# Holding attention visits back while both chains of a product pair are open

## The chip, the cores and the metric

The kernel runs on one core of one Trainium2 chip. The metric is the device time of one execution in microseconds (us); lower is better. A core has five engines that run their own instruction streams side by side: TensorE (PE, the matrix products; its weight loads are listed apart as PEld), VectorE (DVE), ScalarE (ACT), GpSimd (POOL) and SyncE (SP, here a queue of transfers). They wait for each other through semaphores. What stands first in an engine's stream is run first: an instruction that waits holds up everything behind it on its engine.

## The reference

Squared-ReLU attention over 8 batches of 12 heads, 448 rows of 64, then a Fourier mixing with a residual, a normalization, and a feed-forward block (FFN) with a residual:

```python
scores = scale * np.matmul(q, k.transpose(0, 1, 3, 2))
attn = np.maximum(scores, 0.0) ** 2 / S
x = np.matmul(attn, v)                 # then heads side by side: 448 x 768 for each batch
mixed = np.real(np.fft.fft(np.fft.fft(x, axis=1), axis=2))
u = x + mixed
un = (u - mean) / np.sqrt(var + 1e-06)
out = u + np.maximum(un @ w_ch1, 0.0) @ w_ch2      # 768 -> 3072 -> 768
```

## The kernel before

Nothing in this kernel is written in its final order. Each stage is a Python generator that asks a planner (`Streams.run`, L102) for a piece of work: an engine, a duration, what it depends on, which buffers it takes and, if it likes, a condition `ok`. The planner keeps its own clock for each engine and always emits the request that can start first. A request whose condition does not hold sorts behind all that are free to go. It is still emitted when nothing else can be, and, once the FFN is two batches in (`sch.fill`, L2183), also where the best TensorE request would otherwise start over 0.5 planned us later than it. So a condition moves work; it is no wait on the chip. The result is a fixed order of instructions on each engine, with semaphores for the true dependencies alone.

The stages that matter here:

- **Attention** (`attention`, L834) comes as visits to TensorE. A full visit makes one head pair's value product from squared scores (seven matmuls, L822 and L827) and three blocks of new scores (six matmuls, L954). Each score block lies in one of three two-bank PSUM tiles (`BS`, psS), is read by ScalarE (L967, ReLU) and then squared by VectorE (L984) or ScalarE (L981). The values leave PSUM through VectorE or ScalarE into xT (L689, L686).
- **Mixing** of a finished batch: the channel transform (L1432), the row transform (L1240), and behind them sums, statistics and normalization on VectorE, ScalarE and POOL (L1275, L1284, L1303 on ScalarE or L1300 on POOL), stores, and transposed loads of the normalized rows (unT, L1380) on the SP queue.
- **FFN**, by groups of 256 rows from the fourth group on. The first product (L1930) runs as twelve blocks of twelve matmuls; each block fills one of the two remaining PSUM banks (`BF`, psF), which comes free when ScalarE (L1917) or VectorE (L1915) has applied the ReLU. The second product of a row pair saves one product in eight by sums and differences (`Pair`, L2031) and runs as **two chains**, `chain_a` (L2098) and `chain_b` (L2124), each a row of products of twelve matmuls (L2071) into one psF bank. Between two products of a chain, VectorE adds the bank to an output tile (L1623), and the next product of that chain waits for this addition. With both chains open, one runs its product while the other's addition is under way. Both psF banks are then held, so a visit's value product takes a psS tile, and the visit is cut to two score blocks. `chains[0]` counts the open chains: up by one in `first` (L2075) when a chain has its bank, down by one when it is through.
- The last four groups of 256 rows run as two joint stages (`joint`, L1733, products L1762), after the last attention visit; they have their own chains.

What sets the place of a visit is `gate` (L861). `progress[0]` is the FFN's position in batches, and `lead` the position that it must have reached before this visit: that of the visit less 2.9 batches, with a slope (L859, L860). From batch 2 on there must also be 1.3 us of planned FFN work between two visits with scores (`APART`).

Of the kernel before, what the change touches and what calls it, by code (L numbers as in the profile page):

```python
# [149 lines left out]
def need(eng, dur, deps=(), bufs=(), ok=None):  # L150
    return eng, dur, list(deps), list(bufs), ok


def mm(n):
    return n / 2400 + (0.002 if STAGE[0] else 0.006)
# [22 lines left out]
def kernel(  # L178
# [384 lines left out]
    progress, worked, visited = [0.0], [0.0], [-9.0]  # L563
    APART = 1.3
# [79 lines left out]
    tail = [0]  # L644
# [156 lines left out]
    chains, last_values = [0], Cell()  # L801

    def items(m):

        at = m // 2 * 7
        return [at, at + 1, at + 2, at + 3] if m % 2 == 0 else [at + 3, at + 4, at + 5, at + 6]

    def past(sets):

        return sets // 2 * 7 + sets % 2 * 3  # L810

    def turned_for(b, i):

        g, r = divmod(i, 7)
        return turned_at[b][g] if r == 3 else [turned_at[b][g][r > 3]]

    def value(av, i, m, sqs, start, stop, e):

        r = i % 7
        sq, _, home = sqs[i]  # L820
        if r == 3:
            nc.tensor.matmul(av[:, 0:S], lhsT=vn_home[:, (3 * H + 2 * m) * Dh:(3 * H + 2 * m + 2) * Dh], rhs=sq[:, m % 2, :], start=start, stop=stop,  # L822
                             skip_group_check=True)
        else:
            for h in range(2):
                at = (3 * (2 * m + h) + r % 4) * Dh
                nc.tensor.matmul(av[h * Dh:(h + 1) * Dh, 0:S], lhsT=vn_home[:, at:at + Dh], rhs=sq[:, h, :],  # L827
                                 start=start, stop=stop, skip_group_check=True)
        if r != 3 or m % 2:
            sqs.pop(i)  # L830
            sq_ids.append((e, home))
            BSQ.free.append(e)

    def attention(b, left=None):  # L834

        F, sqs, fresh = [], {}, []
        if b == ONE:
            yield need("ACT", 0.0, [], [BSQ] * 3)
            sq_left.t = max(t for t, i in sq_ids if i >= NSQ - 3)
            sq_ids[:] = [(t, i) for t, i in sq_ids if i < NSQ - 3]  # L840
        room = NSQ if b < ONE else NSQ - 3
        p = pa = pv = 0
        while pv < MC:
            if p == NB and pv == MC - 1 and 2 <= b < B - 1 and turned_at[b + 1][0][0].t is not None:
                return F, sqs
            few = b == 0 or progress[0] == 0.0
            n = min(1 if few else 3, NB - p)
            ma = pv

            lag = 3 if few else 1  # L850
            old = fresh[-lag] if len(fresh) >= lag else 0
            values = items(pv)[-1] < old if n else True
            n = max(0, min(n, room - (p - past(pv + values))))
            values = values or not n
            bv, mv, Fv, sv = b, ma, F, sqs
            if left is not None:
                values, bv, mv, (Fv, sv) = True, b - 1, MC - 1, left
            deps, bufs, dur, homes = [], [], 0.0, BF
            lead = b + ((p if n else pa) - (0 if left is None else 4)) / NB  # L859
            lead -= LEAD - SLOPE * (B - lead)  # L860
            gate = lambda: progress[0] >= lead and (b < 2 or worked[0] >= visited[0] + APART) and (b != 1 or tail[0] == 2 or tail[0] == 0 and p < 0)  # L861
            if values:
                deps += [sv[i][1] for i in items(mv)]
                if b > 1:
                    yield need("PE", 0.0, deps, [], gate)
                    if chains[0] == 2:
                        homes, n = BS, min(n, 2)
                bufs.append(homes)
                if b == 1:
                    deps.append(first_mixed)  # L870
                deps.append(ready[bv * NG + mv // 2][2])
                dur += 4 * mm(S) + SWITCH
            fresh.append(p + n)
            if n:
                now = sorted(range(p, p + n), key=lambda i: i % 7 == 3)
                deps += [c for i in now for c in turned_for(b, i)]
                bufs += [BS] * n
                last = [sum(1 + (j % 7 == 3) for j in now[x + 1:]) * mm(S) for x in range(n)]
                dur += (n + (now[-1] % 7 == 3)) * mm(S) + SWITCH
            e = yield need("PE", dur + SWITCH, deps, bufs, gate)  # L880
            av_end, scs = None, []
            if n:
                visited[0] = worked[0]

            for part in ("scores", "values") if few else ("values", "scores"):
                if part == "values" and values:
                    held = homes.take()
                    av = held[:, 0] if homes is BS else held
                    give = lambda when, homes=homes, held=held: homes.give(held, when)
                    order = sorted(items(mv), key=lambda i: i % 7 != 3)  # L890
                    for i in order:
                        value(av, i, mv, sv, i == order[0], i == order[-1], e)
                    av_end = e - (last[0] + mm(S) + SWITCH if n and not few else 0.0) + LATENCY["PE"]
                    if mv % 2 == 1:
                        BQ[2].free.append(e)
                    if bv == B - 1 and mv == MC - 1:
                        last_values.t = e + LATENCY["PE"]
                    if left is None:
                        pv += 1
                        pa = past(pv)  # L900
                if part == "values":
                    continue
                for x, i in enumerate(now if n else []):
                    sc = score(b, i)
                    scs.append((i, sc, e - SWITCH - (4 * mm(S) + SWITCH if values and few else 0.0) - last[x]))
                    if i % 7 == 6:
                        BQT.free.append(e)
            p += n
            for i, _, _ in scs:
                sqs[i] = [None, Cell(), None]  # L910
            if scs:
                sch.add(squares(b, scs, sqs), (0.2, 0.2))
            if av_end is not None:
                left = None
                yield from fold(bv, mv, Fv, av, give, av_end)
# [29 lines left out]
    def score(b, i):  # L945

        g, r = divmod(i, 7)
        qT, flat, (step, apart) = turned[b][g]
        sc = BS.take()
        for h in range(2):  # L950
            ps = slice(0, 128) if r == 3 else slice(h * Dh, (h + 1) * Dh)
            pair = h if r == 3 else r // 4
            k0 = r % 4 * step + pair * apart
            nc.tensor.matmul(sc[:, h, 0:S].rearrange("k (c q) -> k c q", c=4), lhsT=flat[ps, k0:k0 + KB],  # L954
                             rhs=qT[ps, pair], start=True, stop=True)
        return sc
# [519 lines left out]
    def mixes():  # L1476
        for b in range(B):
            yield from mix(b)
# [128 lines left out]
    def ffns():  # L1607
        for b in range(JOINTS[0]):
            yield need("SP", 0.0, [group_ready[b]])
            yield from ffn(b)  # L1610
        for n in range(len(JOINTS)):
            yield from joint(n)
# [544 lines left out]

    LEAD, MIXED, SPARE, ELASTIC = 2.9, 1, 0.5, (1, 99)
    SLOPE = 0.127
    with tc.manual_schedule():  # L2160
        small_constants()
        sch.engine.update(POOL=0.5, DVE=2.6)

        sch.add(loading(), (0, 4))
        sch.add(build_dft(), (0, 0.5))
        sch.add(turning((0,)), (0.05, 0.15))
        sch.add(ffns(), (4, 0))
        sch.add(mixes(), (1, 1))
        sch.add(first_attention(), (0, 0))
        for i in range(2):  # L2170
            sch.add(first_channels(i, range(MC - 1)), (5, 5))
        sch.add(attentions(), (3, 3))
        sch.add(warming(), (9, 9))
        sch.add(weight_sums(), (6, 6))
        sch.add(quarter_sums(), (6, 6))
        sch.add(halve(), (3, 3))
        sch.add(turns(), (1, 1))
        sch.add(turn_rest(), (2, 2))
        sch.add(root_table(), (0, 0.4))
        sch.add(negative(), (0, 0.35))  # L2180
        for slot in range(6):
            sch.add(outputs(slot), (4, 0))
        sch.fill = lambda: progress[0] > 2.0  # L2183
        sch.run()
# [30 lines left out]
```

## Time and profile before

| | |
|---|---|
| median of three runs | 569.09 us |
| the three runs | 569.48, 569.09, 566.94 us |
| profiled execution, first to last instruction | 566.4 us |
| TensorE busy | 556.5 us (98%), 4171 matmuls |
| VectorE busy | 436.2 us (77%) |
| ScalarE busy | 318.2 us (56%) |
| POOL busy | 195.9 us (35%) |

The profiled execution is one execution; its own length is known as the span alone, which leaves out what lies before its first and after its last instruction. Matmuls are pipelined, so that the listed durations of neighbours overlap: the time that one costs is read from the starts of neighbours. For example, a block of twelve matmuls of 384 columns takes 1.95 us from its start to the start of what follows, though each matmul is listed with 326 ns.

In the rows of the views, `L2071 PE MATMUL psF<-w,hT ... x12` stands for twelve matmuls of line 2071 that write psF and read w and hT; a bracket at the end of a row tells how long the engine was idle before it and what ended that.

### The profile page before, as it was taken

Reading aid. Unit: us, or ns where it says so; the run is one execution under the profiler, and the core shown is the slowest. Engines: PE = TensorE matmul, PEld = TensorE weight load, DVE = VectorE, ACT = ScalarE, POOL = GpSimd, SP = SyncE. Lnnn points to the kernel's source line nnn. Section 1 sums busy time; section 2 is a strip of 40 time slices with the busy share of each in tenths; the row PEclk is TensorE's granted clock in tenths of the full one; section 3 lists DMA queues with packets and bytes.
Section 4 is the critical chain, followed back from the end, with each engine's and each line's share of the span. In section 5 each row is a group of like instructions: output and inputs, shape, how many; then the busy total and the mean of one; then the engine's idle time right before and its main releaser. Section 6 shows DMA issues by size and latency. Waiting matters only on the chain.

```text
span 566.4 us, 11147 instructions
## 1 busy us (share of the span) xinstructions
PE 556.5 (98%) x4171; PEld 350.1 (62%) x4171; DVE 436.2 (77%) x1016; ACT 318.2 (56%) x536; POOL 195.9 (35%) x281
## 2 busy tenths in 40 slices
PE   7999999999999999999999999999999999999997
PEld 4376556544465455556756757767678688668864
DVE  7976564987789978887997896888899957644762
ACT  5978762676745686585786637638515154015400
POOL 8966225523346234462545545222015000000000
PEclk9999999999999999999999999999999999999999
DMA  9999999979959988899899979956425421231012
GB/s 110 180 209 230 215 215 165 217 144 134 181 96 210 215 117 179 164 187 184 174 163 196 198 121 198 164 123 154 115 65 174 124 75 29 71 127 56 1 57 83
DMA packets 152688, 82.41 MB, mean 146 GB/s; under 512 B 118076, under 2 KB 147900, under 8 KB 152636
## 3 DMA queue, kind: packets, MB, share of 16 engines
q0 software_dynamic: 57056, 33.63, 43.0%
q1 hardware_dynamic: 95580, 48.09, 38.1%
q8 instruction: 32, 0.52, 0.4%
q14 instruction: 20, 0.16, 0.1%
HBM read 62.91 MB, written 26.25 MB: 157 GB/s over the span
## 4 chain that ended last, share of the span: by engine, by line
PE 86%; DMA 5%; DVE 4%; ACT 2%; POOL 1%; issue 1%; DVEq 0%; POOLq 0%; ACTq 0%
PE psF L1930 25%; PE psF L2071 20%; PE psS L1762 8%; PE psS L954 7%; PE psS L2071 5%; DMA kn<-in_k_dram 5%; PE psF L827 5%; PE psF L1985 4%; PE psS L1432 2%; PE psF L1762 2%; PE psF L1958 2%; PE psF L822 1%; PE psF L623 1%; DVE sq L984 1%; PE psS L827 1%
## 5 line engine op out<-in xcount | busy, mean ns | idle before, releaser
L1930 PE MATMUL psF<-unT,w 128*128 128x256 bf16 (+2 forms) x1152 | 165.3, 299 | 0.0
L967 ACT ACTIVATE sq<-psS 128x896 bf16<-128x896 f32 x168 | 144.1, 919 | 31.7 <-PE psS L954 31.2
L1930 PEld LDWEIGHTS <-w 128*128 128x128 bf16 x1152 | 110.9, 98 | 49.6 <-issue 5.2
L984 DVE TENSOR_TENSOR sq<-sq 128x896 bf16<-128x896 bf16 x144 | 88.9, 634 | 13.3 <-ACT sq L967 12.5
L2071 PEld LDWEIGHTS <-hT 128*128 128x128 bf16 x648 | 62.5, 98 | 44.1 <-issue 4.8
L1917 ACT ACTIVATE hT<-psF 128x512 bf16<-128x512 f32 (+2 forms) x121 | 59.6, 508 | 41.1 <-PE psF L1930 40.3
L1623 DVE TENSOR_TENSOR o<-psF,o 128x384 f32<-128x384 f32 (+1 forms) x78 | 42.6, 547 | 24.3 <-PE psF L2071 20.8
L2071 PE MATMUL psF<-w,hT 128*128 128x384 bf16 x336 | 59.7, 326 | 0.6 <-DVE o L1623 0.6
L954 PE MATMUL psS<-qkT 64*128 64x448 bf16 (+1 forms) x336 | 51.5, 354 | 1.0 <-DVE qkT L630 0.8
L1777 ACT COPY copies<-psS 128x256 f32<-128x256 f32 x57 | 19.9, 374 | 53.0 <-PE psS L1762 48.1
L689 DVE TENSOR_SCALAR xT<-psF 128x224 bf16<-128x224 f32 x60 | 20.6, 384 | 26.1 <-PE psF L827 26.1
L1275 POOL TENSOR_TENSOR u<-tp,xn 112x385 f32<-112x385 f32 (+2 forms) x14 | 14.5, 1037 | 72.6 <-DVE tp L1255 48.6
L476 POOL DMA_DIRECT2D qn<-in_q_dram x21 | 15.7, 747 | 57.7 <-DVE qkr L583 50.3
L827 PE MATMUL psF<-sq,vn 128*64 128x448 bf16 x246 | 33.0, 362 | 0.0
L954 PEld LDWEIGHTS <-qkT 64*128 64x128 bf16 (+1 forms) x336 | 12.9, 94 | 32.3 <-issue 26.4
L1762 PEld LDWEIGHTS <-w 128*128 128x128 bf16 x288 | 28.2, 98 | 4.7 <-issue 1.1
L451 POOL DMA_DIRECT2D kn<-in_k_dram x42 | 25.9, 626 | 10.3 <-DMA w<-in_moe_w_ch_dram 6.0
L1284 DVE BATCH_NORM_STATS2 stats<-u 112x6 f32<-112x384 f32 (+2 forms) x56 | 28.7, 543 | 0.8 <-POOL u L1275 0.6
L451 POOL DMA_DIRECT2D vn<-in_v_dram x42 | 26.1, 638 | 6.2 <-DMA w<-in_moe_w_ch_dram 5.4
L476 POOL DMA_DIRECT2D vn<-in_v_dram x24 | 18.9, 789 | 25.5 <-PE psS L954 25.4
L1303 ACT ACTIVATE un<-u,small 112x768 bf16<-112x768 f32 (+2 forms) x22 | 22.0, 1023 | 9.5 <-DVE small L1290 8.4
L1782 DVE CUSTOM_DVE_ANT_0 hT<-psS,copies 128x256 bf16<-128x256 f32 x37 | 15.0, 421 | 14.1 <-PE psS L1762 6.2
(238 smaller groups left out, 946.9 us busy)
## 6 DMA issues: line engine op xcount, KB each, us to landing
out_dram<-o SPq DMA_DIRECT2D x55, 192.0 KB, 2.3
qn<-in_q_dram POOLq DMA_DIRECT2D x21, 224.0 KB, 5.1
vn<-in_v_dram POOLq DMA_DIRECT2D x24, 192.0 KB, 5.6
w<-in_moe_w_ch_dram POOLq DMA_DIRECT2D x12, 384.0 KB, 11.8
w<-in_moe_w_ch_dram POOLq DMA_DIRECT2D x4, 1152.0 KB, 23.4
kn<-in_k_dram POOLq DMA_DIRECT2D x21, 192.0 KB, 5.9
utop<-u SPq DMA_DIRECT2D x12, 336.0 KB, 2.9
o<-utop SPq DMA_DIRECT2D x16, 192.0 KB, 3.7
```

Of the source, the lines that this page charges most:

```text
L451: nc.gpsimd.dma_start(out=t[par * Dh:(par + 1) * Dh, par::2], in_=at)
L476: nc.gpsimd.dma_start(out=to, in_=src[b, hs, 0:rows].rearrange("h (p j) d -> p h (j d)", j=j))
L827: nc.tensor.matmul(av[h * Dh:(h + 1) * Dh, 0:S], lhsT=vn_home[:, at:at + Dh], rhs=sq[:, h, :], start=start, stop=stop, skip_group_check=True)
L954: nc.tensor.matmul(sc[:, h, 0:S].rearrange("k (c q) -> k c q", c=4), lhsT=flat[ps, k0:k0 + KB], rhs=qT[ps, pair], start=True, stop=True)
L967: nc.scalar.activation(r, sc[:, :, 0:S], AF.Relu)
L984: nc.vector.tensor_tensor(r, r, r, op=ALU.mult)
L1284: nc.vector.bn_stats(stats[:n, hf, :], u[:n, hf * (D // 2):(hf + 1) * (D // 2)])
L1623: nc.vector.tensor_tensor(o[:, cols], pc[:, cols], o[:, cols], op=ALU.add)
L1762: nc.tensor.matmul(ps[:, 0:N], lhsT=lhs, rhs=rhs[:, m], start=(start and m == 0), stop=(stop and m == 2), skip_group_check=True)
L1917: nc.scalar.activation(hs, ps, AF.Relu)
L1930: nc.tensor.matmul(ph[:, i * N:(i + 1) * N], lhsT=w1_sb[m][hf][:, (jj + i) * 128:(jj + i + 1) * 128], rhs=unT[:, m, 0:N], start=(m == 0), ...
L2071: nc.tensor.matmul(pc[:, cols], lhsT=lhs[i], rhs=rhs[i][:, cols], start=(start and i == 0), stop=(i == KP - 1), skip_group_check=True)
```

## The change

The condition gets one more clause. From batch 2 on a visit is also held back while two chains are open, unless the FFN has gone 0.15 batches past the position that the visit needs, that is, unless the visit is late.

```diff
-            gate = lambda: progress[0] >= lead and (b < 2 or worked[0] >= visited[0] + APART) and (b != 1 or tail[0] == 2 or tail[0] == 0 and p < 0)
+            gate = lambda: (progress[0] >= lead and (b < 2 or worked[0] >= visited[0] + APART)
+                            and (b != 1 or tail[0] == 2 or tail[0] == 0 and p < 0)
+                            and (b < 2 or chains[0] < 2 or progress[0] >= lead + LATE))
...
     SLOPE = 0.127
+    LATE = 0.15
```

No instruction is new, and lines after L861 move down by two. The order of TensorE is the same through its first 2070 matmuls and differs from there on, in some places up to the end.

The first place where it differs, on TensorE, in the second product of a group: rows of L2071 are products of the chains (the first row of each twelve, psF_3995 is chain A's bank), L822 begins a value product and L954 a run of scores. Before:

```order
L2071 MATMUL psF_4050<-w2_0_976,hT_883 128x384
L954 MATMUL psS_4064<-qkT_3703 128x448
L2071 MATMUL psF_3995<-wsum_1784,s2_2067 128x384
L2071 MATMUL psF_4114<-wsum_1709,hT_883 128x384
L822 MATMUL psS_4134<-sq_4110,vn_120 128x448
L954 MATMUL psS_4142<-qkT_3703 128x448
L2071 MATMUL psF_4114<-hT_883 128x384
L2071 MATMUL psF_3995<-w2_0_976,s1_2066 128x384
```

Now:

```order
L2073 MATMUL psF_4050<-w2_0_976,hT_883 128x384
L956 MATMUL psS_4071<-qkT_3703 128x448
L2073 MATMUL psF_4088<-wsum_1709,hT_883 128x384
L2073 MATMUL psF_3995<-wsum_1784,s2_2067 128x384
L2073 MATMUL psF_4088<-hT_883 128x384
L822 MATMUL psS_4155<-sq_4112,vn_120 128x448
L956 MATMUL psS_4163<-qkT_3703 128x448
L2073 MATMUL psF_3995<-w2_0_976,s1_2066 128x384
```

Chain B's two products (psF_4114, now psF_4088) were one short visit apart; now a whole product of chain A stands between them, and the visit comes behind both, still while both chains are open.

The second place is TensorE in the first product of the group that starts at 344.4 us before. Rows of L1930 are the last block ahead of a visit; four, four and two blocks lay ahead of the three visits before, and two behind the last; two, two, two and four lie ahead of four visits now, and two behind the last. Before:

```order
L1930 MATMUL psF_4881<-unT_3273,w1_0_0_477 128x256
L822 MATMUL psF_4895<-sq_4864,vn_120 128x448
L954 MATMUL psS_4903<-qkT_4397 128x448
L1930 MATMUL psF_4961<-unT_3273,w1_0_1_585 128x256
L822 MATMUL psF_4982<-sq_4864,vn_120 128x448
L954 MATMUL psS_4990<-qkT_4699 128x448
L1930 MATMUL psF_5036<-unT_3273,w1_0_1_585 128x256
L954 MATMUL psS_5059<-qkT_4699 128x448
L1930 MATMUL psF_5089<-unT_3273,w1_0_1_585 128x256
L2071 MATMUL psF_5108<-w2_0_976,hT_883 128x384
```

Now:

```order
L1932 MATMUL psF_4839<-unT_3273,w1_0_0_477 128x256
L822 MATMUL psF_4863<-sq_4818,vn_120 128x448
L956 MATMUL psS_4871<-qkT_4463 128x448
L1932 MATMUL psF_4905<-unT_3273,w1_0_0_477 128x256
L822 MATMUL psF_4924<-sq_4818,vn_120 128x448
L956 MATMUL psS_4932<-qkT_4690 128x448
L1932 MATMUL psF_4968<-unT_3273,w1_0_0_477 128x256
L956 MATMUL psS_4991<-qkT_4690 128x448
L1932 MATMUL psF_5065<-unT_3273,w1_0_1_585 128x256
L822 MATMUL psF_5083<-sq_5046,vn_120 128x448
L956 MATMUL psS_5091<-qkT_4690 128x448
L1932 MATMUL psF_5127<-unT_3273,w1_0_1_585 128x256
```

The stretch had three visits with seven score blocks and two value products; it now has four with eleven and three, and behind its last block the mixing of a batch (L1432), which stood in the second product before.

The third place is TensorE at the end of attention: the last value products (L822), the chains around them, and the start of the last batch's mixing (L1432). Before:

```order
L822 MATMUL psF_5636<-sq_5614,vn_120 128x448
L954 MATMUL psS_5644<-qkT_5284 128x448
L2071 MATMUL psF_5661<-w2_0_976,hT_883 128x384
L2071 MATMUL psF_5683<-w2_0_976,hT_883 128x384
L822 MATMUL psS_5695<-sq_5614,vn_120 128x448
L2071 MATMUL psF_5661<-wsum_1784,s2_2067 128x384
L2071 MATMUL psF_5725<-wsum_1709,hT_883 128x384
L1432 MATMUL psS_5787<-chan0_114,fold_5577 114x193
```

Now:

```order
L822 MATMUL psF_5649<-sq_5545,vn_120 128x448
L1932 MATMUL psF_5660<-unT_3273,w1_0_1_585 128x256
L2073 MATMUL psF_5678<-w2_0_976,hT_883 128x384
L2073 MATMUL psF_5700<-w2_0_976,hT_883 128x384
L2073 MATMUL psF_5678<-wsum_1784,s2_2067 128x384
L1434 MATMUL psS_5734<-chan0_114,fold_5426 114x193
L2073 MATMUL psF_5776<-wsum_1709,hT_883 128x384
```

The last value product came inside the pair of chains and comes one block of the first product ahead of it now; the last batch's mixing starts 36 matmuls earlier.

Over the whole program, from the first difference on: value products 14 before and 14 now; runs of scores 17 and 18, of which those that stand alone, with no value product ahead of them, 4 and 5. Value products in a psS tile, which are those made while both chains are open: 7 of all before, 8 now. Some small work changes its engine: three ReLUs (L1917 to L1915) and two copies of values, four instructions (L686 to L689), from ScalarE to VectorE, two squares (L984 to L981) from VectorE to ScalarE, three normalizations of 113 rows (L1300 to L1303) from POOL to ScalarE.

## The prediction

> **What bounds the kernel now.** I read the page first, then TensorE's waits, then busy time by stretches, then the order in time at the places where the two programs differ. The page:
>
> ```profile
> span 566.4 us, 11147 instructions
> PE 556.5 (98%) x4171; PEld 350.1 (62%) x4171; DVE 436.2 (77%) x1016; ACT 318.2 (56%) x536; POOL 195.9 (35%) x281
> PEclk9999999999999999999999999999999999999999
> PE 86%; DMA 5%; DVE 4%; ACT 2%; POOL 1%; issue 1%; DVEq 0%; POOLq 0%; ACTq 0%
> ```
>
> TensorE is busy for 98% of the span at the full granted clock, and 86% of the chain that ended last is TensorE. Busy could hide slow matmuls, so I look at how fast they follow each other:
>
> ```profile
> 339.53 2.12 PE L2071 MATMUL psF<-w,hT 128*128 128x384 bf16 x12
> 341.49 2.11 PE L2071 MATMUL psF<-hT 128*128 128x384 bf16 x12
> 343.54 1.03 PE L954 MATMUL psS<-qkT 64*128 64x448 bf16 x6
> 344.41 5.40 PE L1930 MATMUL psF<-unT,w 128*128 128x256 bf16 x48
> 349.65 0.35 PE L822 MATMUL psF<-sq,vn 128*128 128x448 bf16 x1
> ```
>
> Twelve products of a chain take 341.49 - 339.53 = 1.96 us, and a block of the first product (349.65 - 344.41) / 4 = 1.31 us. These are the steps of an unbroken stream. What is left to win after the first difference (289.5 us) is what TensorE still waits there, in the view of waits from 289 us on and in the stretches:
>
> ```profile
> PE psS L1762 <- DVE hT L1782: 0.5, 2, 0.3
> PE psF L2071 <- DVE o L1623: 0.2, 1, 0.2
> ...
> core 0: us, PE busy (x) PEld busy (x) DVE busy (x) ACT busy (x) POOL busy (x), PEclk, DMA share, GB/s
> 289.50:566.40 276.90, 272.31 (x2102) 193.35 (x2101) 205.64 (x475) 121.15 (x234) 55.76 (x63) 1.00 0.54 114
> 382.20:404.90 22.70, 22.70 (x197) 16.03 (x196) 19.50 (x47) 18.28 (x30) 4.94 (x5) 1.00 0.60 145
> 506.70:566.40 59.70, 55.31 (x432) 41.64 (x430) 30.98 (x80) 16.29 (x48) 0.00 (x0) 1.00 0.18 57
> ```
>
> The waits come to 0.7 us. Of 276.90 us TensorE is not busy for 4.59, and 4.39 of these lie in the last stretch, after the last attention visit; most of them are the output's way out behind the last matmul. So between 289.5 and 506.7 us, where visits are moved, 0.2 us of idle time stands against 217 us of work. A change that removes no matmul can hardly gain there.
>
> **The change part by part.** The profile knows nothing of the clause itself: it adds no instruction and no semaphore, only another order. I cost four things.
>
> *The wait that goes.* In the first place of order shown above, chain B's two products had one short visit between them:
>
> ```profile
> 294.76 0.35 PE L822 MATMUL psS<-sq,vn 128*128 128x448 bf16 x1
> 295.05 0.76 PE L827 MATMUL psS<-sq,vn 128*64 128x448 bf16 x6
> 295.74 0.36 PE L954 MATMUL psS<-qkT 64*128 64x448 bf16 x2
> 295.75 0.51 DVE L1623 TENSOR_TENSOR o<-psF,o 128x384 f32<-128x384 f32 x1
> 296.31 2.11 PE L2071 MATMUL psF<-hT 128*128 128x384 bf16 x12 [0.21 <-DVE o L1623]
> ...
> 249.44 0.36 PE L954 MATMUL psS<-qkT 64*128 64x448 bf16 x2
> 249.74 2.12 PE L2071 MATMUL psF<-wsum,hT 128*128 128x384 bf16 x12
> ```
>
> The addition started at 295.75, 0.99 us after chain B's product had ended, because VectorE had other work ahead of it. A score block of two matmuls costs 0.30 us elsewhere (249.44 to 249.74) and cost 0.57 here: 0.27 us lost. Now 1.96 us of chain A stand there, and the addition, late by as much, would end at 295.75 + 0.51 = 296.26, 1.50 us after the product: covered. Term: -0.27. Bounds: 0, if VectorE is later by another 0.5, and -0.27.
>
> *One more run of scores alone.* There are five now for four before. What one costs more than scores behind a value product:
>
> ```profile
> 289.50 1.04 PE L954 MATMUL psS<-qkT 64*128 64x448 bf16 x6
> 290.38 0.65 PE L2071 MATMUL psF<-w,hT 128*128 128x384 bf16 x3
> ...
> 333.49 0.74 PE L954 MATMUL psS<-qkT 64*128 64x448 bf16 x6
> 334.17 1.15 PE L2071 MATMUL psF<-w,s 128*128 128x384 bf16 x6
> ```
>
> Alone 290.38 - 289.50 = 0.88, behind values 334.17 - 333.49 = 0.68, and the product ahead of a lone run takes 343.54 - 341.49 = 2.05 for 1.96: together 0.29. Term: +0.29. Bounds 0.2 to 0.6 (twice that, if other small splits cost as well).
>
> *Crowding in the first product.* The second place has visits two blocks apart. Blocks alternate over two psF banks, so block n + 2 waits for the ReLU of block n, and ScalarE serves ReLUs and scores in one line:
>
> ```profile
> L967 ACT ACTIVATE sq<-psS 128x896 bf16<-128x896 f32 x168 | 144.1, 919 | 31.7 <-PE psS L954 31.2
> L1917 ACT ACTIVATE hT<-psF 128x512 bf16<-128x512 f32 x70 | 41.9, 598 | 29.3 <-PE psF L1930 28.8
> ...
> 398.83 2.54 ACT L967 ACTIVATE sq<-psS 128x896 bf16<-128x896 f32 x3 [0.49 <-PE psS L954]
> ```
>
> The tightest case is the lone run of scores and the four blocks behind it. From the start of the run, scores take 0.88 and the blocks start at 0.88, 2.19, 3.50 and 4.81. ScalarE begins with the ReLU of the block ahead (0.60, to some 0.8), two of the scores (2.54 / 3 = 0.85 each, to 2.5), the ReLU of the first block (to 3.1), the third score (to 3.95), the ReLU of the second (to 4.55). The third block needs a bank at 3.50 and has it at 3.1; the fourth at 4.81 and has it at 4.55. It fits with about 0.25 to spare. That such density runs is seen before: 382.2 to 404.9 held four value products and twelve score blocks in twelve blocks, and TensorE was busy for 22.70 of 22.70. Term: 0. Bounds: 0 and the first rival's price. If that cover goes, each visit costs what ScalarE is late.
>
> *Work that changes engine.*
>
> ```profile
> L984 DVE TENSOR_TENSOR sq<-sq 128x896 bf16<-128x896 bf16 x144 | 88.9, 634 | 13.3 <-ACT sq L967 12.5
> L689 DVE TENSOR_SCALAR xT<-psF 128x224 bf16<-128x224 f32 x60 | 20.6, 384 | 26.1 <-PE psF L827 26.1
> L1915 DVE TENSOR_SCALAR hT<-psF 128x512 bf16<-128x512 f32 x14 | 9.6, 689 | 1.7 <-PE psF L1930 1.5
> L686 ACT ACTIVATE xT<-psS 128x224 bf16<-128x224 f32 x4 | 1.2, 350 | 0.0
> L981 ACT ACTIVATE sq<-sq 128x896 bf16<-128x896 bf16 x24 | 22.8, 960 | 0.4
> L1303 ACT ACTIVATE un<-u,small 113x768 bf16<-113x768 f32 x9 | 9.0, 1025 | 7.3 <-DVE small L1290 7.3
> 308.22 2.48 SPq L1380 DMA_TRANSPOSE unT<-ntop  x1
> ```
>
> VectorE: 3 x 0.689 + 4 x 0.384 - 2 x 0.634 = +2.3 us, with 276.90 - 205.64 = 71 us free. ScalarE: 2 x 0.960 + 3 x 1.025 - 3 x 0.598 - 4 x 0.350 = +1.8 us, with 156 free. POOL loses three instructions. A visit takes with it the transposed loads of its xT and the loads of the next heads on POOL's queue; behind these on SP stand the loads of unT, 2.48 us each, which are issued a whole group ahead of their first product in both orders. Nothing waits for them. The joint stages get other places for some products in other banks; their two waits (0.5 us) may go or double. Term 0, bounds -0.5 and +0.7.
>
> Sum: 566.4 - 0.27 + 0.29 = **566.4 us** for the profiled execution: no change. The median of the runs shown, 569.09, stands 2.7 us above that span; I add the same and forecast **569.1 us**. By the bounds the best is -0.27 + 0.2 - 0.5 = -0.6 and the worst without a rival 0.6 + 0.7 = +1.3, so 568.5 to 570.4 for this case, and 567 to 571 with the spread of the runs.
>
> **The rivals.** *Crowded visits make ScalarE late (slower).* Place: the first products of the three groups from 303.8 us on, with eleven visits now. Were ScalarE 0.65 late at each, by a normalization of 1.025 us or a score ahead of the ReLU (0.85 to 1.03, less the 0.25 to spare, is 0.6 to 0.8), this would cost 11 x 0.65 = 7.2 us; at six of the eleven 3.9, which makes 573.0. It decides from five on. For it: ScalarE was busy for 18.28 of 22.70 us in the densest stretch. Against it: that stretch lost nothing, and the work there is as dense as now.
>
> *The unprofiled runs lose time in the chains, and the clause removes it (faster).* The three runs lie 2.5 us apart and up to 3.1 over the span. Were 569.09 - 566.94 = 2.15 us of that waits of chain products behind late additions, and these and all 0.7 us of waits gone, the time would be 569.09 - 2.15 - 0.7 = 566.2. Against it: the trace shows no such wait but the one of 0.27, and an unbroken stream on TensorE elsewhere.
>
> *The clause does not do what it says.* It is a preference of the planner, and late visits pass. Value products in a psS tile, those inside two open chains, number 8 now and 7 before, so it keeps none out in sum; it only shuffles. Then the time is 569.1 as well, give or take the reshuffling.
>
> *TensorE cools down.* Visits that are held could leave TensorE idle, and the granted clock with it. The row of the clock shows no slice below 9, and its longest wait after 289 us is 0.3 us; a chain left alone would wait for one addition, 0.51 us in the row above. Were the clock to halve for one run of four blocks, it would cost another 5.24 us: 574.3. The Trainium skill (TensorE: Matmul & The Clock Gate, "Why this matters for your kernels") warns of idle gaps over about 3 us between bursts, after which the clock falls to half; by that rule the gaps here are too short, and the trace agrees, with the full clock throughout.
>
> **How the numbers follow.** The forecast has 0.57, the clause without effect 0.12, crowding 0.20, the faster rival 0.09, the clock 0.02. About 0.5% (2.8 us) is what a measurement of this kernel can tell from no change. The first two are within it: 0.69. Slower are crowding and the clock: 0.22. Faster: 0.09. The range reaches from 566.2 (the faster rival) to 572.8 (crowding at five to six visits).
>
> **What would show it.** In the profile of the changed kernel: at the first place, the wait of L2073 (psF, hT) for the addition is gone; in the first product of the group from about 344 us TensorE's stretch is unbroken, with no idle time at L1932 put down to L1919 or L1917 of the ReLU (crowding would show it there); lone runs of scores cost some 0.9 us; the last batch's mixing starts some 6 us earlier (36 matmuls, three products of a chain) and nothing behind it ends earlier, since the joint stages wait for the products ahead of them; TensorE stays at 98% and the clock full. The forecast is wrong if TensorE's waits from 289 us on exceed 3 us, or if they are as short as before and the runs still differ by more than 0.5%.

## The result

| | before | changed |
|---|---|---|
| median of ten runs each | 567.97 us | 569.40 us |
| lowest to highest | 566.94 to 569.48 | 569.19 to 571.51 |
| profiled execution, span | 566.4 us | 568.8 us |
| TensorE busy | 556.5 us | 558.2 us |

The ratio is 1.0031 (95% interval 1.0017 to 1.0044): slower by 0.3%, which lies inside the 0.5% that I had called no change. The page of the changed kernel's profile, the lines that answer to those shown of before:

```profile
span 568.8 us, 11132 instructions
PE 558.2 (98%) x4171; PEld 350.3 (62%) x4171; DVE 438.0 (77%) x1021; ACT 320.6 (56%) x534; POOL 190.3 (33%) x278
PEclk9999999999999999999999999999999999999999
```

The same matmuls at the same full clock, and 2.4 us more span. The view of TensorE's waits from 289 us to the last matmul, and the stretches:

```profile
PE psS L1764 <- DVE hT L1784: 0.6, 2, 0.3
PE psF L2073 <- DVE o L1625: 0.5, 1, 0.5
PE psS L1764 <- ACT copies L1779: 0.4, 2, 0.2
PE psS L2073 <- DVE hT L1784: 0.3, 1, 0.3
PE psS L1764 <- DVE o L1625: 0.2, 1, 0.2
```

```profile
core 0: us, PE busy (x) PEld busy (x) DVE busy (x) ACT busy (x) POOL busy (x), PEclk, DMA share, GB/s
289.50:303.80 14.30, 13.76 (x90) 6.91 (x88) 12.26 (x32) 11.32 (x16) 8.83 (x13) 1.00 1.15 180
344.10:367.20 23.10, 23.10 (x203) 16.99 (x202) 19.56 (x41) 17.24 (x27) 5.67 (x8) 1.00 1.11 183
```

The waits come to 2.0 us where before had 0.7. One of them (L2073, psF, for the addition of L1625) stands at the first place of order and is 0.54 us; the other 1.5 us stand in the joint stages (L1764, and L2073 into psS). The group from 344 us, where the visits were crowded, has none: TensorE is busy for 23.10 of 23.10 us.

A wait's length is not what it costs, so I compare when the same matmul starts. Three marks cut the program: the last unchanged block at 280 us, the start of the next group at 304 us, behind the first place, and the first joint product. Each mark is one row of the order in time; the third, of before and of the changed kernel:

```profile
451.55 1.15 PE L1762 MATMUL psS<-unT,w 128*128 128x256 bf16 x9
```

```profile
452.43 1.15 PE L1764 MATMUL psS<-unT,w 128*128 128x256 bf16 x9
```

| us between the marks | 280 to 304 | 304 to joints | joints to end |
|---|---|---|---|
| before | 23.42 | 147.73 | 114.85 |
| changed | 23.86 | 148.22 | 116.32 |
| difference | +0.44 | +0.49 | +1.47 |

The first 280 us of these two agree within 0.05. (Over the profiled executions below whose program is the same there, they take 279.83 to 280.94 us, so the span of one execution tells nothing below 1 us; the two spans here lie 2.4 us apart, the medians 1.4.) So there are three losses to explain, and the largest is one for which I had put down zero.

**The first place.** In the order in time of the changed kernel, TensorE:

```profile
289.95 1.04 PE L956 MATMUL psS<-qkT 64*128 64x448 bf16 x6
291.53 2.11 PE L2073 MATMUL psF<-wsum,hT 128*128 128x384 bf16 x12 [0.54 <-DVE o L1625]
```

and VectorE at the same time:

```profile
288.58 1.43 DVE L986 TENSOR_TENSOR sq<-sq 128x896 bf16<-128x896 bf16 x1
289.93 0.54 DVE L1279 TENSOR_TENSOR u<-tp,xn 112x383 f32<-112x383 f32 x1
290.40 0.61 DVE L986 TENSOR_TENSOR sq<-sq 128x896 bf16<-128x896 bf16 x1
290.93 0.54 DVE L1625 TENSOR_TENSOR o<-psF,o 128x384 f32<-128x384 f32 x1
```

Chain B's first product ends where the scores start, at 289.95. Its bank is the one that chain B's next product needs, so that product waits for the addition. The addition stands behind a square, a sum for u and another square, starts 0.98 us after the product and ends at 291.47. The lone run of scores covers 0.88 us of this (289.50 to 290.38 in before); TensorE resumes at 291.53, 0.7 us after the scores. Before, three matmuls of chain B and a product of chain A stood behind the same scores and covered it.

**The joint stages.** Rows of the order in time with a wait, in the changed kernel:

```profile
481.53 0.49 PE L1764 MATMUL psS<-chan,w 128*128 128x256 bf16 x3 [0.25 <-DVE o L1625]
510.94 0.49 PE L1764 MATMUL psS<-chan,quarter 128*128 128x256 bf16 x3 [0.29 <-DVE hT L1784]
512.27 0.49 PE L1764 MATMUL psS<-chan,quarter 128*128 128x256 bf16 x3 [0.19 <-ACT copies L1779]
521.77 0.49 PE L1764 MATMUL psS<-chan,quarter 128*128 128x256 bf16 x3 [0.18 <-ACT copies L1779]
529.74 0.27 PE L1764 MATMUL psS<-chan,quarter 128*128 128x256 bf16 x1 [0.27 <-DVE hT L1784]
531.83 1.62 PE L2073 MATMUL psS<-w,hT 128*128 128x384 bf16 x9 [0.29 <-DVE hT L1784]
```

and in before:

```profile
514.83 0.81 PE L1762 MATMUL psS<-sumx,w 128*128 128x256 bf16 x6 [0.30 <-DVE hT L1782]
536.02 0.49 PE L1762 MATMUL psS<-chan,w 128*128 128x256 bf16 x3 [0.19 <-DVE hT L1782]
```

Measured from start to start, against the step of an unbroken stream, a row of this kind costs some 0.16 us more than its bracket says. Counting every step that is over 0.15 us too long, the changed kernel has six gaps there with 2.45 us in all, before has four with 1.17.

### The profile page after: what moved, and what is told of

Same layout as the page of the kernel before. It is cut to its first block, busy times and chain, and to the rows that moved or that the text cites. A ratio compares the mean times of both kernels' runs of the same rounds, so it can differ in the third digit from the quotient of the medians.

```text
span 568.8 us, 11132 instructions
## 1 busy us (share of the span) xinstructions
PE 558.2 (98%) x4171; PEld 350.3 (62%) x4171; DVE 438.0 (77%) x1021; ACT 320.6 (56%) x534; POOL 190.3 (33%) x278
## 4 chain that ended last, share of the span: by engine, by line
PE 81%; DMA 7%; DVE 4%; ACT 2%; POOL 2%; issue 2%; SPq 1%; DVEq 0%; POOLq 0%; ACTq 0%
PE psF L1932 22%; PE psF L2073 19%; PE psS L956 7%; PE psS L2073 7%; PE psS L1764 7%; DMA qn<-in_q_dram 6%; PE psF L827 4%; PE psF L1987 4%; PE psF L1764 2%; PE psS L1434 2%; PE psF L1960 2%; PE psF L822 1%; PE psS L827 1%; DMA out_dram<-o 1%; DVE sq L986 1%
## 5 line engine op out<-in xcount | busy, mean ns | idle before, releaser
L986 DVE TENSOR_TENSOR sq<-sq 128x896 bf16<-128x896 bf16 x142 | 87.2, 632 | 10.5 <-ACT sq L969 10.0
L2073 PEld LDWEIGHTS <-hT 128*128 128x128 bf16 x648 | 62.6, 98 | 44.9 <-issue 5.3
L1919 ACT ACTIVATE hT<-psF 128x512 bf16<-128x512 f32 (+2 forms) x118 | 57.8, 505 | 42.0 <-PE psF L1932 41.2
L1625 DVE TENSOR_TENSOR o<-psF,o 128x384 f32<-128x384 f32 (+1 forms) x73 | 39.7, 546 | 18.2 <-PE psF L2073 14.6
L2073 PE MATMUL psF<-w,hT 128*128 128x384 bf16 x294 | 51.9, 326 | 0.6 <-DVE o L1625 0.6
L1779 ACT COPY copies<-psS 128x256 f32<-128x256 f32 x48 | 17.3, 375 | 56.0 <-PE psS L1764 28.4
L1277 POOL TENSOR_TENSOR u<-tp,xn 112x385 f32<-112x385 f32 (+2 forms) x14 | 14.3, 1024 | 79.5 <-DVE tp L1257 46.5
L689 DVE TENSOR_SCALAR xT<-psF 128x224 bf16<-128x224 f32 x58 | 19.8, 383 | 23.4 <-PE psF L827 23.4
L956 PEld LDWEIGHTS <-qkT 64*128 64x128 bf16 (+1 forms) x336 | 12.8, 94 | 32.2 <-issue 26.7
L1764 PEld LDWEIGHTS <-w 128*128 128x128 bf16 x288 | 28.2, 98 | 4.3 <-issue 0.4
L1305 ACT ACTIVATE un<-u,small 113x768 bf16<-113x768 f32 (+2 forms) x25 | 25.1, 1024 | 3.6 <-DVE small L1292 2.4
L1784 DVE CUSTOM_DVE_ANT_0 hT<-psS,copies 128x256 bf16<-128x256 f32 x40 | 16.3, 421 | 13.2 <-ACT copies L1779 7.1
```

The lines of the kernel that those rows point to most:

```text
L986: nc.vector.tensor_tensor(r, r, r, op=ALU.mult)
L1625: nc.vector.tensor_tensor(o[:, cols], pc[:, cols], o[:, cols], op=ALU.add)
L1764: nc.tensor.matmul(ps[:, 0:N], lhsT=lhs, rhs=rhs[:, m], start=(start and m == 0), stop=(stop and m == 2), skip_group_check=True)
L1919: nc.scalar.activation(hs, ps, AF.Relu)
L2073: nc.tensor.matmul(pc[:, cols], lhsT=lhs[i], rhs=rhs[i][:, cols], start=(start and i == 0), stop=(i == KP - 1), skip_group_check=True)
```

## The experiments

All are compared with the kernel before, run beside them on the same chip (its median was 567.8 to 568.0 each time). "Late" is against before at the same matmul.

**E1: the changed visits, the old joint order.** From the first joint stage on, the planner's own choice is replaced by the list of choices that it made in the kernel before (the lines that hold the list and name each piece of work are left out here):

```diff
                 key = (ok is not None and not ok(), max(t) + HEAD.get((s[3], eng, phase), 0.0), s[1][eng != "PE"])
+                if self.joined:
+                    key = (False, ORDER.get(f"{s[4]}/{s[5]}", -1.0), 0)
```

> The visits of the changed kernel, the joint stages' order of the kernel before (each pick from the first joint stage on replayed, so TensorE has its products and banks there as before). In the changed kernel's profile TensorE is 0.88 us late when the joint stages begin (452.43 against 451.55) and 2.35 us late at the end. Theory JOINT ORDER (the other 1.47 us come from the reshuffled joint products): 0.9 us late at the joint start and still 0.9 at the end; span 566.4 + 0.9 = 567.3, ratio to before 1.0016. Theory STATE (the loss in the joint stages comes from what the visits leave behind on the other engines, whatever the order): 2.3 us late at the end, 568.7, ratio 1.003. Theory SPREAD (the joint stages differ by 1.5 us between executions of one kernel): anything from 0.9 to 2.4, and the repeat of the changed kernel beside it differs from its first profile as much.

**E2: the old visits, the changed joint order.** The same edit in the kernel before, with the list of the changed kernel.

> The visits of the kernel before, the joint stages' order of the changed kernel. JOINT ORDER: nothing late at the joint start (451.5), 1.5 us late at the end, span 567.9, ratio to before 1.0026. STATE: like the kernel before throughout, 566.4, ratio 1.000. SPREAD: between the two, and not repeated from one execution to the next.

**E3: the clause without its first place.**

```diff
-                            and (b < 2 or chains[0] < 2 or progress[0] >= lead + LATE))
+                            and (b < 2 or chains[0] < 2 or progress[0] >= lead + LATE or progress[0] < 3.43))
```

> The clause without its first place: it is off until the FFN's progress is 3.43 batches, past the one product pair (281 to 303 us) where the order first changes; TensorE's order is that of the kernel before up to its 2993rd product, some 407 us. Theory FIRST PLACE (the uncovered product of chain B and the lone run of scores cost the 0.7 us that TensorE is late at 344 us): none of it here, TensorE at 344.4 and 406.0 as before, ratio 1.000 plus what its own joint order costs, 0 to 1.5 us. Theory OTHER PLACES (the loss comes at every held visit, not at one): 0.2 to 0.9 us late at the joint start, ratio 1.001 and more.

**The changed kernel again**, without an edit.

> The changed kernel again, beside the three others on one chip. If its loss is in its order: 0.4 us late at 298 us, 0.7 at 344, 0.9 at 452, 2.3 at the end, each within 0.2, ratio 1.003. SPREAD: the part in the joint stages (1.47 us) differs by 0.5 us or more from the first profile.

What the four gave:

| | ratio to before (95%) | 280 to 304 | 304 to joints | joints to end |
|---|---|---|---|---|
| before | 1 | 23.42 | 147.73 | 114.85 |
| changed again | 1.0051 (1.0034 to 1.0068) | 23.86 | 147.92 | 116.33 |
| E1 | 1.0017 (1.0006 to 1.0029) | 23.86 | 147.93 | 114.86 |
| E2 | 1.0038 (1.0024 to 1.0052) | 23.36 | 147.73 | 117.31 |
| E3 | 1.0044 (1.0028 to 1.0060) | 23.35 | 147.74 | 117.00 |

In these runs the segments repeat to 0.01 us where the order is the same, so SPREAD is out but for two pieces. Of the 0.49 us between 304 us and the joints in the first profile, 0.30 did not come back in the repeat, in E1, or later. It is one gap of 0.29 us at 322.5 us, within a first product, in one execution. And the stretch from 280 to 304 us has two lengths for one order: before's order took 23.41 or 23.42 us in three executions (before, E5, E6) and 23.35 or 23.36 in four (E2, E3, E9, E10), the changed one 23.86 in three and 23.53 in E7. What goes with that is in the last section.

JOINT ORDER is right: with the old list the joint stages take 114.86 us as before, whatever the visits did (E1), and with the changed list they are long though the visits are old (E2). I had expected E2 to lose 1.5 us there; it lost 2.46. The rows that make the difference, in E2's order in time:

```profile
453.68 0.55 DVE L1745 TENSOR_TENSOR sumx<-unT,chan 128x768 bf16<-128x768 bf16 x1
454.62 1.08 DVE L1822 CUSTOM_DVE_ANT_0 hT<-psS,copies 128x256 bf16<-128x256 f32 x3
455.08 0.49 PE L1802 MATMUL psS<-chan,quarter 128*128 128x256 bf16 x3 [0.94 <-DVE hT L1822]
```

The changed order fits its own visits: when its first joint product starts, at 452.43, VectorE has begun all four differences of rows that the first joint stage needs, the last (sumx) at 451.62. In E2 the first joint product starts at 452.02, all four come behind this point, and L1822, for which the product waits, comes behind them. Joined to the old visits, the list waits once more. So STATE is not wholly wrong: an order costs more behind a state of the other engines for which it was not made.

FIRST PLACE is right for the visits: E3 is level with before up to the joints. It is no better in the end. There the planner chose for itself, and TensorE's joint order came out as in the changed kernel, matmul for matmul; behind before's visits it meets the wait of E2 again (0.63 us) and takes 117.00. On TensorE E3 differs from before, up to the joint stages, only in the last pair of chains: the last visit comes three matmuls later, still inside the pair, and the products behind it change places. That is enough to turn the joint order over.

**E4: two neighbours on VectorE exchanged.** In the changed kernel's list of choices one line is moved up, nothing else:

```diff
 chain_b b3 c0/1
+chain_b b3 c0/2
...
 square b5 #16/0
-chain_b b3 c0/2
```

> The changed kernel with two neighbours on VectorE exchanged and nothing else: chain B's first addition (290.67 us in the repeat's trace) stands ahead of the square before it (290.14). Theory LATE ADDITION (TensorE's new wait at the first place, a gap of 0.71 us, is the addition standing behind VectorE's other work): the addition starts at about 290.14, TensorE's next product 0.53 us earlier, the gap falls from 0.71 to about 0.18, and all behind it up to the joint stages is 0.5 us earlier. Theory ROUND TRIP (the product needs the bank, the bank needs the addition, and the addition the product ahead: too short a cover whatever VectorE does first): the gap stays at 0.5 us or more. Time: -0.5 us against the changed kernel by the first, 0 by the second.

In E4's order in time, VectorE:

```profile
289.57 0.55 DVE L1398 TENSOR_TENSOR u<-tp,xn 112x383 f32<-112x383 f32 x1
290.21 0.56 DVE L1744 TENSOR_TENSOR o<-psF,o 128x384 f32<-128x384 f32 x1
290.68 0.62 DVE L1105 TENSOR_TENSOR sq<-sq 128x896 bf16<-128x896 bf16 x1
```

and TensorE:

```profile
290.11 1.04 PE L1075 MATMUL psS<-qkT 64*128 64x448 bf16 x6
290.98 0.81 PE L2193 MATMUL psF<-wsum,hT 128*128 128x384 bf16 x4
```

From scores to product it is 0.87 us now, for 1.58: LATE ADDITION is right and ROUND TRIP is out. More was won than the 0.53 us expected, because the first square was also shorter in this execution (1.11 us for 1.43, see the last section). Like with like, the exchange is worth 0.54 us where the square takes 1.43 (E8 below: 289.76 to 290.80, 1.04 for 1.58) and 0.20 where it takes 1.10 or 1.11 (E4 against E7, which has the changed order: 290.12 to 291.19, 1.07). From 280 to 304 us E4 takes 23.35, from 304 to the joints 147.93, in the joints 116.32. Time: ratio 1.0025 (1.0001 to 1.0048).

**E5, E6, E7: a larger reserve in the joint stages.** Why has one joint order more gaps than another? The planner adds a reserve to every copy and sum there; I raised it, in before to 0.6 and 0.8, in the changed kernel to 0.8:

```diff
-        d, SLACK, to_go = 3 * mm(N), 0.4, [3 * KP]
+        d, SLACK, to_go = 3 * mm(N), 0.6, [3 * KP]
```

> The kernel before, with the planner's reserve in the joint stages at 0.6 us in place of 0.4 (SLACK in joint()); all up to the first joint stage is as before. Before has 4 gaps over 0.15 us on TensorE there, 1.17 us in all, the changed kernel 6 with 2.45. Theory TIGHT PLAN (the gaps come because the planner lets a product follow too closely on the copy or sum that frees its bank; the order of the changed kernel happens to have two more of them): a larger reserve takes most of the gaps away, 0 to 0.6 us of them left, joint stages 0.5 to 1.2 us shorter than before. Theory LOTTERY (any nudge of the order there gives another set of gaps, with no trend): 1 to 3 us of gaps, more or less than before.

> The kernel before with that reserve at 0.8 us, above every gap seen in the joint stages (0.46 at most). TIGHT PLAN: at most one gap left, 1 us shorter than before. LOTTERY: 1 to 3 us of gaps.

> The changed kernel with the reserve at 0.8 us. TIGHT PLAN: the joint stages lose 1.5 to 2.4 us against the changed kernel, which is then as fast as before or 0.5 us behind (what its visits cost stays). LOTTERY: 1 to 3 us of gaps, no better on the whole than with 0.4.

**E9, E10: a smaller reserve**, 0.2 and 0 in the kernel before, after these had fallen.

> The kernel before with the reserve in the joint stages at 0.2 us. With 0.6 and 0.8 the joint stages took 4 us longer than with 0.4, with 11 gaps for 4. Theory TRUE TIMES (the planner goes best where its times are nearest to the real ones: in the trace a copy starts 0.19 us after its product and the next product can follow some 0.05 us after the copy, while the planner counts 0.68 and 0.58 with a reserve of 0.4): fewer gaps with less reserve, joint stages 114.0 to 114.8 us against 114.85. LOTTERY: 115 to 119 us, no trend; 0.4 was a lucky draw among these.

> The kernel before with no reserve in the joint stages. TRUE TIMES: the fewest gaps of all, joint stages 113.7 to 114.5 us. LOTTERY: 115 to 119 us.

| reserve, visits | joints to end, us | gaps over 0.15 us, their sum | ratio to before (95%) |
|---|---|---|---|
| 0, before (E10) | 120.36 | 16, 6.0 us | 1.0129 (1.0088 to 1.0169) |
| 0.2, before (E9) | 118.58 | 10, 4.2 us | 1.0071 (1.0042 to 1.0100) |
| 0.4, before | 114.85 | 4, 1.2 us | 1 |
| 0.6, before (E5) | 118.87 | 11, 4.9 us | 1.0072 (1.0050 to 1.0093) |
| 0.8, before (E6) | 118.88 | 11, 5.0 us | 1.0050 (1.0034 to 1.0065) |
| 0.4, changed | 116.32 | 6, 2.5 us | 1.0031 (1.0017 to 1.0044) |
| 0.8, changed (E7) | 118.79 | 11, 5.0 us | 1.0070 (1.0047 to 1.0093) |

TIGHT PLAN and TRUE TIMES both fall: more reserve makes more gaps, less reserve makes more gaps too, and 0.4 is the best of five. TensorE's waits from the joint stages on in E6, where the reserve is twice as large:

```profile
PE psS L1762 <- ACT copies L1777: 2.0, 4, 0.7
PE psS L1762 <- DVE o L1623: 0.5, 1, 0.5
...
```

The larger reserve did not keep products away from copies here; it made the planner choose otherwise. LOTTERY comes nearest, though it had the sizes too small: 1 to 3 us of gaps, where 4.2 to 6.0 came. The runs hold six joint orders of TensorE in all (before's, the changed kernel's, one each of E5, E9 and E10, and one that E6 and E7 share), and before's is the best: the others are 1.5 to 5.5 us longer. Why it is the best is not settled by this; a reserve that was chosen by trying would look like that, and so would chance.

**E8: both causes taken away.** E4's exchange and E1's joint order together.

> The changed kernel with both found causes taken away: the exchange of the two VectorE instructions, and the joint stages' order of the kernel before. The visits stay as the clause puts them. Theory TWO CAUSES (the late addition 0.7 us and the joint order 1.47 us are all that the change costs): from 280 us on the repeat of the changed kernel lost 0.63 us up to the joint stages and 1.47 in them; this one loses -0.1 and 0.0, ratio to before 1.000, within 0.0015. Rival MORE (something else at the visits costs time in unprofiled runs): ratio 1.0015 or above though the trace is level with that of before.

23.33, 147.92 and 114.86 us between the marks, 286.11 in all against 286.00 in before. Ratio 1.0008 (0.9995 to 1.0022). TWO CAUSES holds in the trace to 0.1 us and in the time within its interval, which a rest of up to 0.2% would also fit. The visits that the clause moved remain in E8, and cost 0.19 us behind the first place.

**E11: the clause without its exception.**

```diff
-    LATE = 0.15
+    LATE = 99
```

> The clause without its exception (LATE = 99 in place of 0.15): from batch 2 on, a visit waits whenever both chains are open, however far it is due; the order now differs from some 180 us on. Theory ACCIDENT (holding visits costs nothing by itself; what costs is a product whose addition comes late by chance, and a new draw of the joint order): 0 to 1.5 us late when the joint stages begin, those then anywhere from 115 to 120 us. Rival CROWDING (held visits pile up behind the chains and make ScalarE late, so more holding costs more): over 2 us late at the joint start, spread over waits of L1932 and L956 for ScalarE in the groups from 180 us on.

Ratio 1.0317 (1.0266 to 1.0367), span 584.0 us. The joint stages begin at 467.96, 16.4 us late, and take 116.05, in before's order once more, with one wait of 0.90 us for VectorE that before lacks. Neither theory gave this: ACCIDENT is out, and CROWDING has the size but not the cause. TensorE's waits in E11 from 170 us to the joint stages:

```profile
PE psF L1932 <- DMA unT<-ntop: 6.4, 1, 6.4
PE psS L956 <- DMA qkT<-qkr: 2.9, 2, 1.8
PE psF L2073 <- DVE o L1625: 2.2, 4, 0.6
PE psF L2073 <- DVE xT L689: 0.7, 1, 0.7
PE psF L822 <- ACT hT L1919: 0.6, 1, 0.6
```

Of 12.8 us of waits ScalarE is the cause of 0.6; before waits 0.9 us there in all, so the waits make 11.9 of the 16.4 us. The largest is a chain of transfers. In E11's order in time:

```profile
258.18 0.53 SPq L1340 DMA_DIRECT2D ntop<-un  x1
263.39 1.86 SPq L1382 DMA_TRANSPOSE unT<-ntop  x1
269.24 1.04 PE L1932 MATMUL psF<-unT,w 128*128 128x256 bf16 x4 [6.39 <-DMA unT<-ntop]
```

and in before's:

```profile
246.50 0.40 SPq L1338 DMA_DIRECT2D ntop<-un  x1
253.47 3.06 SPq L1380 DMA_TRANSPOSE unT<-ntop  x2
262.80 1.47 PE L1930 MATMUL psF<-unT,w 128*128 128x256 bf16 x12
```

Held visits finish a batch's attention late; its mixing stores the normalized rows 11.7 us later, the transposed loads are issued 9.9 us later, and the next group of the FFN waits for them. Most of the rest is the clock: E11 is the only one of these traces in which the granted clock falls within the work, twice. Stretches of E11 (their last three figures are the clock, the DMA share and GB/s):

```profile
267.15:273.98 6.83, 4.74 (x23) 3.38 (x24) 0.00 (x0) 0.60 (x1) 0.00 (x0) 0.50 1.02 223
332.00:335.42 3.42, 3.42 (x17) 2.19 (x15) 1.52 (x5) 1.73 (x2) 1.99 (x4) 0.50 0.97 190
```

It falls to 0.50 towards the end of the wait of 6.39 us, and again at 332.00 behind a wait of 1.84 us, which is shorter than the 3 us that the prediction went by. The two blocks at 269.24 take 4.93 us for 2.62. Half of 4.74 and of 3.42 us makes some 4.1 us lost, and with the waits 16.0 of the 16.4. So the exception of 0.15 batches is what keeps the clause nearly harmless. It seldom lets the clause decide: with 0.05 or 0.3 in its place, or with the clause off past a progress of 3.43, the program that comes out is the changed kernel's, instruction for instruction. In the changed kernel the clause decides at one pair, and every other difference follows from it by the planner's choices.

## Why the prediction was right, and where it was wrong

The forecast of 569.1 us, the range and "no change" held; the measured median is 569.4. But the number was hit by luck, with two errors that offset each other. I added 2.7 us to the span because the median of three runs stood that far above it; ten runs put the median at 567.97, and most executions lie 1.8 to 2.0 us above their span. So my zero was 1.1 us too high, and the change, which I put at 0, cost 1.4.

- **The wait that goes (-0.27).** Chain B's second wait did go, and like with like it was worth its 0.27: the new gap of 0.70 less 0.27 is 0.43, and the segment lost 0.44. But one execution had shown me a wait that only some have. Of the seven with before's order there, before, E5 and E6 have it (0.20 or 0.21 us idle); E2, E3, E9 and E10 lose nothing at that visit, where the addition came 0.46 us after the value product's start (295.31 in the row below, product at 294.85) and not 0.99. These four lost 0.2 us earlier, in the product ahead of the lone scores, so that the segment differs by 0.07 at most. In E3:

```profile
294.85 0.35 PE L822 MATMUL psS<-sq,vn 128*128 128x448 bf16 x1
295.31 0.51 DVE L1625 TENSOR_TENSOR o<-psF,o 128x384 f32<-128x384 f32 x1
```

- **Its other side: the step that failed.** I wrote that the late addition was now covered by 1.96 us of chain A. That is true of chain B's second addition. Its first addition lost its cover by the same exchange, and I did not walk it: the order printed above shows chain B's first product, one lone run of scores, and chain B's next product. The numbers were at hand: an addition 0.99 us late plus 0.51 for itself, against 0.88 of scores, gives 0.6 us. Measured 0.7 for the gap and +0.44 net in the segment; E4 and E8 take it away with one exchange. In E7, where VectorE was less late, the same order cost 0.17 us (23.53 for 23.36).
- **One more run of scores alone (+0.29, bounds 0.2 to 0.6).** Behind the first place the moved visits cost 0.19 us in the repeat, E1, E4, E7 and E8 alike. The term has the right sign and is a little too large; that all of the 0.19 is the lone run was not separated.
- **Crowding (0).** Right: 23.10 of 23.10 us busy in the densest group. With it the first rival falls; even E11 shows ScalarE as the cause of 0.6 us alone.
- **Work that changes engine, unT loads, joint stages (0, bounds -0.5 and +0.7).** The joint stages were mis-sized: +1.47, twice the upper bound. I let their waits "go or double" as if they were two fixed events; they belong to a whole order that one moved visit turns over, and the six orders that ran take 114.85 to 120.36 us. The transfers were rightly put at nothing for this change, though the 2.48 us that I gave each load of unT is the longest of them (1.2 to 2.5 us); E11 shows what they cost when their cover goes.
- **The rivals.** The faster one is out: of the 67 runs of before beside the experiments, 61 have spans of 565.1 to 566.7 us, near the profiled 566.4 or below it, so no such waits hide there. "The clause does not do what it says" is nearly right: it decides at one pair. The clock stayed full; that held visits can bring it down is shown by E11 alone.
- **What I had asked to see.** The wait of L2073 is not gone but moved and grown; the group from 344 us is unbroken; the last batch's mixing starts at 412.60 for 417.57, 5.0 us earlier for the 6 foretold, and nothing ends earlier by it; the waits stay under 3 us.

## What to carry to other kernels

When a change moves one product of a chain, walk every addition of that chain, not only the one that was late before: the cover that one gains is taken from another. And where a planner makes the order, price every stage behind the first difference as a new order, with bounds from other orders of that stage, though no condition of the change reaches it; here all five others were slower than the old one. A joint order that is good can be kept by a recorded list, as E1 and E8 did, so that a change upstream is measured by itself.

## What the runs showed of the hardware

VectorE and POOL take turns here. At 286 us each makes half of one sum (L1277), and the two start within 0.03 us of each other. In the changed kernel:

```profile
286.11 1.34 POOL L1277 TENSOR_TENSOR u<-tp,xn 112x385 f32<-112x385 f32 x1 [3.62 <-ACT un L1305]
286.12 0.55 DVE L1277 TENSOR_TENSOR u<-qs,xn 112x385 f32<-112x385 f32 x1
...
288.65 0.86 POOL L1279 TENSOR_TENSOR u<-qs,xn 112x383 f32<-112x383 f32 x1
```

and in E7, which has the same order up to the joint stages:

```profile
286.08 0.91 POOL L1277 TENSOR_TENSOR u<-tp,xn 112x385 f32<-112x385 f32 x1 [3.61 <-ACT un L1305]
286.11 1.30 DVE L1277 TENSOR_TENSOR u<-qs,xn 112x385 f32<-112x385 f32 x1
...
290.12 1.04 PE L956 MATMUL psS<-qkT 64*128 64x448 bf16 x6
291.19 2.11 PE L2073 MATMUL psF<-wsum,hT 128*128 128x384 bf16 x12
```

One of them has its usual time and the other is longer by 0.43 on POOL or 0.75 on VectorE. Before, the changed kernel, its repeat, E1, E5, E6 and E8 show the first outcome, E2, E3, E4, E7, E9 and E10 the second; which one comes is not a matter of the order in the program.

The square of 1.43 us at 288.58 above (0.61 without a neighbour) stood beside POOL's next sum, the last row of the changed kernel here; where POOL had begun 0.24 us ahead of it, in E4 and E7, it took 1.11 and 1.10. The outcome decides both waits at the first place. With the first one before's order has its wait of 0.2 us each time, and the changed order its wait of 0.54; with the second neither shows idle time there. In E7 the addition starts 0.47 us after the product, not 0.98, and TensorE resumes 1.07 us after the start of the scores, not 1.58: 0.5 us of the addition's lateness goes with the outcome. That VectorE is held up by POOL there is read from the sizes; no run changed POOL's work by itself.

The Trainium skill (SBUF — State Buffer, "Who interferes with whom") says that a VectorE instruction with two SBUF inputs contends with a GpSimd instruction that reads SBUF, that the pair of ports they share is an exclusive lock, and that issue order decides who blocks. These rows agree in size, 0.61 + 0.86 = 1.47 for 1.43; in the changed kernel the square that came out long is the one that is recorded as starting first, by 0.07 us, so the recorded start does not tell who holds the lock.
